# Attention and SwiGLU on one core: visits joined, products reordered, a third product in banks of its own

## The chip, the core and the metric

The kernel runs on one core of a Trainium2 chip. The core has a matrix engine (TensorE, PE in the profile), two engines for vectors (VectorE, DVE, and ScalarE, ACT), a general engine (GpSimd, POOL), and a queue engine that only sends DMAs here (SyncE, SP). Products land in PSUM, eight banks that PE writes and VectorE and ScalarE read; everything else is in SBUF. The metric is the time of one execution on the device in microseconds (us), median over several runs. All arithmetic is in float32.

## The reference

Attention without a softmax, then a feed-forward block:

```python
kv = np.einsum('bhsd,bhse->bhde', k, v)            # per batch and head, 64 x 64
out = np.einsum('bhsd,bhde->bhse', q, kv)
rms = np.sqrt(np.mean(out * out, axis=-1, keepdims=True) + 1e-06)
out = out / rms * g_norm
x = out.transpose(0, 2, 1, 3).reshape(B * S, H * D) # 4608 tokens x 512
g = x @ w_gate                                      # 512 x 1536
val = x @ w_val
return (g / (1 + np.exp(-g)) * val) @ w_out         # 1536 x 512
```

There are 8 batches, 8 heads, 576 positions and a head size of 64. q, k and v are float32; the three weights arrive as 64-bit numbers.

## The kernel before

**Blocks.** The 4608 tokens are nine blocks of 512. Block n lies across batches n-1 and n, so its attention needs the kv of both. Blocks 0, 1 and 2 are computed one at a time (`alone`), blocks 3 to 8 in pairs (`Pair`). Block 0 loads and converts the weights as it goes and multiplies plainly (`plain_up`). From block 1 on, each large product is split into 2 x 2 quarters and computed as seven products of quarter size with sums around them (a Strassen scheme in Winograd's form); the numbers 1 to 7 in the code name these products. In the pairs the seven are split once more (`Inner`).

**Up and Down.** `Ffn.up` (line 1094) makes the gate and value products for block 1 and block 2. It has six units, one for each pair of weight columns (`Up`, j = 0 to 5), and unit j's last two products, 3 and 4, are done within unit j+1; `sequence` (line 700) gives that order. The last unit has no successor: `end` (line 733) does its 3 and 4. `Ffn.down` (line 1118) then does the seven products with w_out, in the order of line 1122, and between them the attention of the next block (`steps`). For the last pair, blocks 7 and 8, there is no next block. In `Up` a product is 8 matmul instructions (a float32 matmul is two of them), in `Down` 24.

**Banks.** Products go to three PSUM pools. `CHAIN` (line 629) tells which: 1, 6, 7 and 4 add up in one bank of b, 5 and 3 in one bank of c, 2 has a bank of a. After each product a method copies or adds the running sum out (`after1`, `after6` and so on; ScalarE copies b, VectorE adds a and c), and the next product on the same bank waits until that is done. a has one bank, b three, c two. The remaining pool, m_psum, has two banks and serves attention. `Up.after7` (line 709) first copies b on ScalarE and then lets VectorE add c to the copy; the Silu of the other half stands behind that copy on ScalarE.

**Attention beside the products.** A visit is a stretch of 64 x 64 matmuls put between two products. `kv` (line 359) multiplies k by v for one or two groups of heads: 72 matmul instructions a group. `heads` (line 423) multiplies q by kv; `half(i)` in `ahead` (line 1269) does 64 of them. In block 1's Up, `third` and `two_thirds` visit block 2's two groups after products (1, 7) and (3, 7), where (j, p) is unit j and product p. In block 2's Up, `ahead` (line 1253) prepares blocks 3 and 4: both groups of block 3 after (0, 1), group 0 of block 4 after (1, 7), block 3's half 0 after (2, 1) and half 1 after (3, 1), and group 1 of block 4 after (3, 7).

**Loads.** k, v and q of the blocks ahead share four tiles (`ld_pool`), so a load waits until an earlier tile has been used. `load_kv(g)` is four DMAs of 288 KB on SyncE, `load_quarters` 16 small ones for half of q. `ffn.sends` is a list of which up to ten are sent after each product. `place_x` (line 515) writes the transposed x by 16 DMAs; for block 2 half of these are ScalarE's.

**Order.** A scheduler orders the instructions of each engine when the kernel is built, by the program's order and its own estimate of when each is ready; it may bring one forward. It also gives out the buffers. `in_order` fixes the program's order: for PE in the whole of block 2 and in the pairs' Down, and for VectorE and ScalarE in block 2's Up. PE in block 1 and in the pairs' Up is left to the scheduler. `tc.issue_after(x)` puts what is inside behind x on x's engine.

**Pairs.** `Inner` has four groups g of products for each j. A copy (line 825) or an add takes each product out. `made3` (line 845) ends a j: it multiplies the two halves of h, and applies a Silu to the second one (line 854) between; it runs inside the next j's first group. `Pair.second_sums` makes sums of h for the second block on GpSimd while the first block is in Down.

**The end.** In Down, product 3 comes last and adds onto 5 in bank c. For block 8 (`self.final`) its two halves have separate banks, the halves are stored one after the other, and product 4's result is stored before.

Of the kernel before, what the change touches and what calls it, by code (L numbers as in the profile page):

```python
# [14 lines left out]
P = 128  # L15
# [3 lines left out]
def kernel(  # L19
# [210 lines left out]
    class Att:  # L230
# [125 lines left out]
                    )  # L356
                self.q.append(tile_.rearrange("p (j u) d -> p j (u d)", u=2))

        def kv(self, g, apart=False):


            if self.n == B:
                return
            if g == 0 or apart:
                self.kv_ps = [m_psum.tile([P, 2, D], F32, name="m") for _ in range(2)]
            for c in range(KT):
                for r in range(2):
                    k, v = self.k[2 * g + r], self.v[2 * g + r]
                    for u in range(2):
                        self.positions = nc.tensor.matmul(  # L370
                            self.kv_ps[r][u * D : (u + 1) * D, g, :], lhsT=k[:, u, c, :], rhs=v[:, u, c, :],
                            start=(c == 0), stop=(c == KT - 1),
                        )
            if g == 1 or apart:
                dst = kvs[self.n % 3].rearrange("p (g r) d -> p r g d", r=2)
                of = slice(g, g + 1) if apart else slice(0, 2)
                for r in range(2):
                    nc.scalar.copy(out=dst[:, r, of], in_=self.kv_ps[r][:, of])
# [304 lines left out]
    class Up(Quad):  # L683
# [14 lines left out]
            self.w = {1: b11, 2: b21, 3: b22, 6: t2, 5: t[0], 7: t[1], 4: t[2]}  # L698

        def sequence(self, last):  # L700
            return [(self, 1), (self, 5), (last, 4), (last, 3), (self, 6), (self, 2), (self, 7)]

        def operands(self, p, e, i):
# [1 line left out]

        def after2(self):
            add(nc.vector, self.s, self.ps["a"], self.s)

        def after7(self):
            self.u3 = self.piece(2)  # L710
            copied = nc.scalar.copy(out=self.u3, in_=self.ps["b"])

            with tc.issue_after(copied.ins):
                nc.scalar.activation(out=self.s, in_=self.s, func=ACT.Silu)
            added = add(nc.vector, self.u3, self.ps["c"], self.u3)

            owed, self.ffn.owed = self.ffn.owed, None
            if owed:
                with tc.issue_after(added.ins):
                    owed()  # L720
# [11 lines left out]

        def end(self):

            for p in (3, 4):
                self.multiply(p)
            self.ffn.ended = self.ffn.h_sums(self.j, 1, nc.vector)

# [13 lines left out]
    class Inner:  # L752
# [50 lines left out]
        def multiply(self, p):  # L803
            if p == 1:
                self.begin()
            name, first = CHAIN[p]
            if first:
                self.ps[name] = PSUMS[name].tile([P, 2, 2, P], F32, name=name)
            ps = self.ps[name][:, 0 : len(self.outers)]
            for i, o in enumerate(self.outers):  # L810
                self.ffn.multiplied = nc.tensor.matmul(  # L811
                    ps[:, i], lhsT=stream.use(self.ffn.n, self.j, o, p), rhs=self.operand(o, p),
                    start=first and i == 0, stop=True, skip_group_check=True,
                )
            if p in self.ADDED:
                e, q = self.ADDED[p]
                dst = self.dst[:, :, :, e, q]
                add(nc.vector, dst, ps, dst)
            else:
                e, q = self.MADE[p]  # L820
                dst = self.dst[:, :, :, e, q]
                if self.onto:
                    add(nc.vector, dst, ps, self.onto(e, q))
                else:
                    nc.scalar.copy(out=dst, in_=ps)  # L825
            if p in (2, 7, 3, 4):
                getattr(self, f"made{self.g}", lambda *_: None)(p, e, q)
            stream.pump()
# [16 lines left out]
        def made3(self, p, e, q):  # L845
            if p != 4:
                return
            h = h_both[:, :, 2 * self.j : 2 * self.j + 2]
            halves = lambda t: t.rearrange("p (b e) t -> p b e t", b=2)
            c11, c12, c21, c22 = (self.whole(*i) for i in ((1, 1), (3, 1), (3, 0), (1, 0)))  # L850

            engine = nc.gpsimd if self.j + 1 < NP else nc.vector
            mul(engine, h[:, :, :, 0:HB], halves(c11), halves(c12))
            nc.scalar.activation(out=c21, in_=c21, func=ACT.Silu)
            mul(engine, h[:, :, :, HB:BLK], halves(c21), halves(c22))
            self.ffn.ended = self.ffn.a.h_sums(self.j, 1, engine)

# [119 lines left out]
    class Down(Quad):  # L977
        def __init__(self, ffn):
            super().__init__(NP)
            self.ffn = ffn  # L980
            self.t = {}
            self.final = ffn.n == NB - 1
            self.opens = None
            self.keeps = False
            if self.final:
                self.apart["c"] = None
# [13 lines left out]
                    )  # L1000
                self.t[p] += [t[:, 0], t[:, 1]]

        def multiply(self, p):
            super().multiply(p)
            if p in self.t and not self.keeps:
                stream.free(("T", p))
            if p == 7 and self.opens:
                stream.enable(self.opens)
            stream.pump()

        def order(self, p):
            order = [(e, i) for e in range(2) for i in range(self.steps)]
# [13 lines left out]
        def turn_s3(self):  # L1026

            pairs = self.ffn.h.rearrange("p (j e) t -> p e j t", e=2)
            sub(nc.vector, pairs[:, 0, :, 0:HB], pairs[:, 0, :, HB:BLK], pairs[:, 1, :, HB:BLK])

        def after2(self):
            add(nc.vector, self.o1[:, :, 0:HD], self.ps["a"], self.s)
            if self.final:
                self.ffn.store(self.o1[:, :, 0:HD], 0, slice(0, HD))

            pairs = self.ffn.h.rearrange("p (j e) t -> p e j t", e=2)
            self.s4 = sub(nc.vector, pairs[:, 1, :, 0:HB], pairs[:, 1, :, 0:HB], pairs[:, 0, :, HB:BLK])

        def after7(self):
            o = ring()  # L1040
            self.o1, self.o2 = o[:, 0:2], o[:, 2:4]
            u3 = self.piece(2)
            nc.scalar.copy(out=u3, in_=self.ps["b"])
            self.add_c(self.o2[:, :, HD:DM], u3)
# [21 lines left out]
    class Ffn:  # L1066
# [51 lines left out]
        def down(self, nxt, then={}):  # L1118

            down = self.down_  # L1120
            fill = nxt.steps() if nxt else {}
            for p in (1, 6, 5, 7, 2, 4, 3) if 5 in fill else (1, 5, 6, 7, 2, 4, 3):
                if p == 1 and 7 not in down.t:
                    down.turn_t(7, self.ended)
                if p == 6 and 4 not in down.t:
                    down.turn_t(4, nxt.halves[0] if nxt and nxt.n >= TURNED else None)

                with tc.issue_after(nxt.multiplied.ins) if self.n == 0 and p in (5, 6) else ExitStack():
                    down.multiply(p)
                self.make(12)  # L1130
                if p in fill:
                    fill[p]()
# [7 lines left out]
                if p == 1:  # L1140

                    with tc.issue_after(nxt.q_turned.ins) if self.n == 0 else ExitStack():
                        down.turn_s3()

        def plain_up(self, f, halves=(0, 1)):

# [95 lines left out]
    load_weights(4)  # L1242
    squared, scaled = blocks[0].first()

    def visit(ffn, att, gs, apart=False):

        with tc.issue_after(ffn.multiplied.ins):
            for g in gs:
                att.kv(g, apart)
        if att.n < B:  # L1250
            ffn.visited = att.positions

    def ahead(ffn, att, then):
# [8 lines left out]
        def turn(i):  # L1262
            ffn.chores.append(lambda: att.turn_q(i))

        def second():
            visit(ffn, then, (0,), True)
            ffn.sends.append(lambda: then.load_kv(1))

        def half(i):
            with tc.issue_after(ffn.multiplied.ins):  # L1270
                att.heads(i, range(NS), (m_psum, m_psum))
            ffn.visited = att.multiplied
            ffn.chores += att.chores(i)
            if i:
                ffn.chores += att.turn_steps()

        def rest():
            for i in range(2):
                load(then, i)()

        def raw():
            for j in range(2, NP):
                ffn.sends += raw_steps(j)

        def sums():
            ffn.chores.extend(att.sum_steps())

        for j in (NP - 2, NP - 1):
            ffn.making.extend(kept_steps(j, chunks(h_alone[:, NF - 4 :]) if j == NP - 1 else chunks(xi_alone)))

        return {
            (0, 1): first, (1, 6): lambda: turn(0), (1, 7): second, (2, 1): lambda: half(0), (2, 6): lambda: turn(1),
            (2, 7): rest, (3, 1): lambda: half(1), (3, 7): lambda: visit(ffn, then, (1,), True), (4, 1): att.place_x,
            (4, 2): raw, (5, 5): att.gain_x, (5, 6): sums,
        }

    def alone(n):
# [27 lines left out]
        elif n == 1:  # L1325

            def third():
                visit(ffn, nxt, (0,))
                nxt.load_kv(1)

            def two_thirds():
                visit(ffn, nxt, (1,))
                for i in range(2):
                    nxt.load_q(i)

            ffn.up({(1, 7): third, (3, 7): two_thirds})
            nxt.turn()
            for g in range(2):
                blocks[PAIRED].load_kv(g)
        else:  # L1340
            with in_order(nc.vector.engine, nc.scalar.engine):
                ffn.up(ahead(ffn, nxt, blocks[PAIRED + 1]))
# [8 lines left out]
            with tc.issue_after(nxt.scaled.ins):  # L1351
                blocks[PAIRED].inner_sums()

        ffn.down(nxt, {7: inner_sums} if n == 2 else {})
        if n == 0:
            blocks[2].load_kv(0)

            with tc.issue_after(nxt.halves[0].ins):
                for j in range(NP // 2):
# [69 lines left out]
```

## Time and profile before

| What | Value |
|---|---|
| Time, median of 3 runs | 1017.61 us (1016.21 to 1017.73) |
| Profiled execution, own time | 1018.16 us |
| its span, first to last instruction | 1016.4 us |
| PE: waits for another engine after 140 us, together | some 5 us |
| Block 1 Up and Down, about | 157 to 272 us |
| Block 2 Up and Down, about | 272 to 392 us |
| Pairs (3, 4), (5, 6), (7, 8) | 392 to 602, 602 to 810, 810 to 1016 us |
| SyncE: transfers on its queue | 138.20 MB, 50.3% of the 16 DMA engines |

The profile describes one execution. Its times are counted from the first instruction. A row of a timeline gives the start, the time until the last of the merged instructions ends, the engine, the line in the kernel, the operation, what it writes and reads, the shape and the count; a bracket says how long the engine stood idle before it and who released it. Many operations are recorded at the line of a small helper (lines 130 to 132 are add, sub and mul), so they are told apart by the tiles they touch. PE's busy time is modelled from a pipeline: two matmuls of one product start 0.216 us apart, though each row says 0.38.

### The profile page before, as it was taken

The page shows a single profiled execution, that of the slowest core. Times are in us where ns is not written, and L with a number is a line of the kernel's source. Part 1 is how long each engine was busy: PE and PEld are TensorE (multiplying, and loading weights), DVE is VectorE, ACT ScalarE, POOL GpSimd, SP SyncE. Part 2 cuts the span into 40 slices and gives each one's busy share as a digit, 9 for nine tenths or more (in the row PEclk, how much of TensorE's full clock was granted, in tenths as well). Part 3 has the DMA queues.
Part 4 walks back from the last instruction along what each step waited for, and adds up shares of the span by engine and source line. Part 5 has one row for each costly group of instructions (what it writes and reads, how often), then busy time and mean ns, then how long its engine had stood idle before and what let it go on. Part 6 is the DMA issues. An engine that isn't in the chain of part 4 may idle for free.

```text
span 1016.4 us, 17091 instructions
## 1 busy us (share of the span) xinstructions
PE 995.9 (98%) x6506; PEld 831.0 (82%) x6506; DVE 665.9 (66%) x1118; ACT 232.5 (23%) x367; POOL 368.3 (36%) x290
## 2 busy tenths in 40 slices
PE   5999999999999999999999999999999999999998
PEld 4544688888888888888888888888888888888887
DVE  2999797759767467656676746666668466666211
ACT  2666111221122211212212121121112121122000
POOL 0000273525444230445456004455660025546600
PEclk9999999999999999999999999999999999999999
DMA  8689643656665845766642364667221655452011
GB/s 220 198 263 270 125 79 132 219 166 145 170 144 109 224 94 157 190 175 176 165 139 43 109 165 133 183 164 191 75 43 42 147 164 154 142 156 84 1 42 42
DMA packets 254290, 143.23 MB, mean 141 GB/s; under 512 B 149504, under 2 KB 236544, under 8 KB 254208
## 3 DMA queue, kind: packets, MB, share of 16 engines
q1 hardware_dynamic: 223488, 138.20, 50.3%
q10 hardware_dynamic: 30656, 3.94, 2.4%
q8 instruction: 52, 0.85, 0.4%
q14 instruction: 30, 0.25, 0.1%
q0 software_dynamic: 64, 0.00, 0.0%
HBM read 104.99 MB, written 28.70 MB: 132 GB/s over the span
## 4 chain that ended last, share of the span: by engine, by line
PE 81%; DVE 8%; DMA 5%; ACT 1%; issue 1%; POOL 1%; SPq 1%; DVEq 0%; POOLq 0%; ACTq 0%
PE b L661 23%; PE b L811 21%; PE c L661 12%; PE c L811 10%; PE a L661 6%; PE a L811 5%; DMA ld<-in_moe_w_out_dram 2%; PE m L431 1%; PE m L370 1%; DVE r L190 1%; DVE arena L131 1%; DVE arena L199 1%; DMA arena<-in_v_dram 1%; SPq L333 1%; POOL t L131 1%
## 5 line engine op out<-in xcount | busy, mean ns | idle before, releaser
L811 PE MATMUL b<-arena,t 128*128 128x256 f32 x1008 | 244.5, 381 | 0.0
L811 PEld LDWEIGHTS b<-arena,t 128*128 128x128 f32 x1008 | 190.0, 190 | 29.6 <-DVE r L130 2.4
L130 POOL TENSOR_TENSOR r<-r 128x256 f32<-128x256 f32 (+1 forms) x90 | 94.8, 1054 | 246.4 <-DMA t<-w 149.4
L130 DVE TENSOR_TENSOR r<-b,r 128x512 f32<-128x512 f32 (+1 forms) x234 | 139.0, 607 | 60.3 <-PE b L811 55.4
L130 DVE TENSOR_TENSOR r<-c,r 128x512 f32<-128x512 f32 (+1 forms) x170 | 104.7, 624 | 108.0 <-PE c L811 41.3
L131 POOL TENSOR_TENSOR t<-wo 128x512 f32<-128x512 f32 x54 | 76.6, 1440 | 175.8 <-DVE wo L130 104.6
L132 POOL TENSOR_TENSOR arena<-r 128x1024 f32<-128x1024 f32 (+1 forms) x54 | 100.8, 1882 | 105.8 <-DVE r L130 81.4
L130 DVE TENSOR_TENSOR r<-a,r 128x512 f32<-128x512 f32 x93 | 59.2, 637 | 110.7 <-PE a L661 73.6
L811 PE MATMUL c<-arena,t 128*128 128x256 f32 x504 | 122.5, 379 | 1.0 <-ACT r L825 0.8
L131 DVE TENSOR_TENSOR arena<-arena 128x512 f32<-128x512 f32 (+3 forms) x96 | 103.2, 1090 | 18.1 <-PE b L661 14.0
L811 PEld LDWEIGHTS c<-arena,t 128*128 128x128 f32 x504 | 95.6, 190 | 14.7 <-ACT r L825 1.2
L661 PE MATMUL b<-wo,arena 128*128 128x256 f32 x432 | 98.3, 382 | 0.4 <-issue 0.3
L661 PE MATMUL b<-t,arena 128*128 128x256 f32 x432 | 96.4, 379 | 1.4 <-POOL s L130 0.7
L661 PEld LDWEIGHTS b<-t,arena 128*128 128x128 f32 x432 | 81.9, 190 | 13.2 <-POOL s L130 1.1
L661 PEld LDWEIGHTS b<-wo,arena 128*128 128x128 f32 x432 | 81.2, 190 | 12.7 <-DVE arena L132 0.9
L825 ACT COPY r<-b 128x512 f32<-128x512 f32 x54 | 31.6, 585 | 191.5 <-PE b L811 191.5
L131 POOL TENSOR_TENSOR t<-arena 128x512 f32<-128x512 f32 x36 | 51.4, 1438 | 59.4 <-DMA w<-t 23.3
L811 PE MATMUL a<-arena,t 128*128 128x256 f32 x252 | 66.1, 379 | 0.0
L811 PEld LDWEIGHTS a<-arena,t 128*128 128x128 f32 x252 | 47.9, 190 | 6.5
L661 PE MATMUL c<-wo,arena 128*128 128x256 f32 x216 | 48.2, 379 | 0.2 <-DVE r L130 0.2
L661 PE MATMUL c<-t,s 128*128 128x256 f32 x216 | 48.1, 379 | 0.0
L661 PE MATMUL a<-wo,arena 128*128 128x256 f32 x216 | 48.1, 379 | 0.0
(105 smaller groups left out, 1224.2 us busy)
## 6 DMA issues: line engine op xcount, KB each, us to landing
t<-w SPq DMA_DIRECT2D x180, 256.0 KB, 3.1
out_dram<-r SPq DMA_DIRECT2D x17, 512.0 KB, 2.9
ld<-in_k_dram SPq DMA_DIRECT2D x26, 288.0 KB, 5.4
ld<-in_v_dram SPq DMA_DIRECT2D x26, 288.0 KB, 5.9
t<-w SPq DMA_DIRECT2D x54, 128.0 KB, 2.2
ld<-in_moe_w_gate_dram SPq DMA_DIRECT2D x12, 512.0 KB, 4.8
ld<-in_moe_w_val_dram SPq DMA_DIRECT2D x12, 512.0 KB, 4.6
ld<-in_moe_w_out_dram SPq DMA_DIRECT2D x12, 512.0 KB, 5.0
```

The source lines that it names most:

```text
L130: add = lambda e, o, a, b: e.tensor_tensor(out=o, in0=a, in1=b, op=OP.add)
L131: sub = lambda e, o, a, b: e.tensor_tensor(out=o, in0=a, in1=b, op=OP.subtract)
L132: mul = lambda e, o, a, b: e.tensor_tensor(out=o, in0=a, in1=b, op=OP.mult)
L190: return nc.vector.scalar_tensor_tensor(out=mag, in0=mag, scalar=3, in1=sign, op0=OP.logical_shift_left, op1=OP.bitwise_xor)
L199: return nc.vector.tensor_tensor(out=dst.bitcast(U32), in0=self.mag.rearrange("p (a b) -> p a b", a=a, b=b), in1=unit.bitcast(U32).rearran ...
L333: queue.dma_start(out=to[32 * r : 32 * (r + 1), j, g0:g1], in_=q[b, 4 * i + 2 * j + h, s0 : s0 + 32 * (g1 - g0), 32 * d : 32 * (d + 1)].re ...
L370: self.positions = nc.tensor.matmul(self.kv_ps[r][u * D : (u + 1) * D, g, :], lhsT=k[:, u, c, :], rhs=v[:, u, c, :], start=(c == 0), stop= ...
L431: self.multiplied = nc.tensor.matmul(self.ps[i][u][p : p + D, t, j, :], lhsT=self.qt[rows, tile_t, head, p : p + D], rhs=kvs[b % 3][rows, ...
L661: self.ffn.multiplied = nc.tensor.matmul(banks[e][:, e], lhsT=lhsT, rhs=rhs, start=first and i == 0 and (e == 0 or banks[0] is not banks[1 ...
L811: self.ffn.multiplied = nc.tensor.matmul(ps[:, i], lhsT=stream.use(self.ffn.n, self.j, o, p), rhs=self.operand(o, p), start=first and i == ...
L825: nc.scalar.copy(out=dst, in_=ps)
```

## The change

1. **Visits joined.** In block 1 both groups of block 2's kv are done in one visit after (1, 7), both groups' k and v are sent for in block 0, and q after that one visit. In block 2, group i of block 4's kv is done directly behind half(i), after (2, 1) and (3, 1), in one bank of a and one of b; k and v of group 1 are sent for after (2, 1).
2. **k and v of block 3** are sent for in two steps: group 0 where both were, group 1 in block 1's Down after product 5, behind `place_x`.
3. **The last weight pair (j = 5)** of blocks 1 and 2: the sequence becomes 1, 5, (last 4), 6, (last 3), 7, 2, and `end` does 4 and then 3. The Silu moves from `after7` to `after2` for this unit.
4. **Blocks 7 and 8** (`lone`): Down's order becomes 1, 5, 6, 2, 7, 3, 4, with product 3 in banks of m_psum. VectorE adds product 5 to u2 after product 6. For block 8, product 3 is cut: its first half before 4, its second half behind it. The output tile is taken in `after2`.
5. **Pairs' Up:** the second Silu of `made3` is put behind the latest ScalarE copy of a product 5 (`fifth`).

```diff
-        def kv(self, g, apart=False):
+        def kv(self, g, apart=False, pools=None):
...
             if g == 0 or apart:
-                self.kv_ps = [m_psum.tile([P, 2, D], F32, name="m") for _ in range(2)]
+                self.kv_ps = [pool.tile([P, 2, D], F32, name=pool.name[0]) for pool in pools or (m_psum, m_psum)]
...
         def sequence(self, last):
+            if self.j == NP - 1:
+                return [(self, 1), (self, 5), (last, 4), (self, 6), (last, 3), (self, 7), (self, 2)]
             return [(self, 1), (self, 5), (last, 4), (last, 3), (self, 6), (self, 2), (self, 7)]
...
         def after2(self):
             add(nc.vector, self.s, self.ps["a"], self.s)
+            if self.j == NP - 1:
+                nc.scalar.activation(out=self.s, in_=self.s, func=ACT.Silu)
...
-            with tc.issue_after(copied.ins):
-                nc.scalar.activation(out=self.s, in_=self.s, func=ACT.Silu)
+            if self.j < NP - 1:
+                with tc.issue_after(copied.ins):
+                    nc.scalar.activation(out=self.s, in_=self.s, func=ACT.Silu)
...
-            for p in (3, 4):
+            for p in (4, 3):
                 self.multiply(p)
...
-                    nc.scalar.copy(out=dst, in_=ps)
+                    copied = nc.scalar.copy(out=dst, in_=ps)
+                    if p == 5:
+                        self.ffn.fifth = copied
...
-            nc.scalar.activation(out=c21, in_=c21, func=ACT.Silu)
+            with tc.issue_after(self.ffn.fifth.ins):
+                nc.scalar.activation(out=c21, in_=c21, func=ACT.Silu)
...
+        def third(self, es):
+
+
+            if es[0] == 0:
+                tiles = [m_psum.tile([P, 2, HB], F32, name="m") for _ in range(1 + self.final)]
+                self.thirds = tiles[0], tiles[-1]
+            for e in es:
+                for i in range(self.steps):
+                    lhsT, rhs = self.operands(3, e, i)
+                    self.ffn.multiplied = nc.tensor.matmul(
+                        self.thirds[e][:, e], lhsT=lhsT, rhs=rhs, start=i == 0 and (e == 0 or self.final),
+                        stop=i == self.steps - 1, skip_group_check=True,
+                    )
+            if not self.final:
+                add(nc.vector, self.o1[:, :, HD:DM], self.thirds[0], self.u2)
+                self.ffn.store(self.o1, 0)
+                return
+            for e in es:
+                add(nc.vector, self.o1[:, e, HD:DM], self.thirds[e][:, e], self.u2[:, e])
+                self.ffn.store(self.o1[:, e : e + 1, HD:DM], e, slice(HD, DM))
+
+        def after6(self):
+            super().after6()
+            if self.lone:
+                self.add_c(self.u2, self.u2)
...
-            for p in (1, 6, 5, 7, 2, 4, 3) if 5 in fill else (1, 5, 6, 7, 2, 4, 3):
+            down.lone = nxt is None
+            order = (1, 6, 5, 7, 2, 4, 3) if 5 in fill else (1, 5, 6, 7, 2, 4, 3)
+            if down.lone:
+                order = (1, 5, 6, 2, 7, 3, 4)
+            for p in order:
...
-                    down.multiply(p)
+                    down.multiply(p, *[(0,)] * (p == 3 and down.lone and down.final))
...
+            if down.lone and down.final:
+                down.multiply(3, (1,))
...
-        def second():
-            visit(ffn, then, (0,), True)
-            ffn.sends.append(lambda: then.load_kv(1))
-
         def half(i):
             with tc.issue_after(ffn.multiplied.ins):
                 att.heads(i, range(NS), (m_psum, m_psum))
-            ffn.visited = att.multiplied
+            visit(ffn, then, (i,), True, (a_psum, b_psum))
             ffn.chores += att.chores(i)
             if i:
                 ffn.chores += att.turn_steps()
+            else:
+                ffn.sends.append(lambda: then.load_kv(1))
...
             def third():
-                visit(ffn, nxt, (0,))
-                nxt.load_kv(1)
-
-            def two_thirds():
-                visit(ffn, nxt, (1,))
+                visit(ffn, nxt, (0, 1))
                 for i in range(2):
                     nxt.load_q(i)
 
-            ffn.up({(1, 7): third, (3, 7): two_thirds})
+            ffn.up({(1, 7): third})
             nxt.turn()
-            for g in range(2):
-                blocks[PAIRED].load_kv(g)
+            blocks[PAIRED].load_kv(0)
...
+        def second_kv():
+            with tc.issue_after(nxt.placed.ins):
+                blocks[PAIRED].load_kv(1)
+
-        ffn.down(nxt, {7: inner_sums} if n == 2 else {})
+        ffn.down(nxt, {1: {5: second_kv}, 2: {7: inner_sums}}.get(n, {}))
         if n == 0:
-            blocks[2].load_kv(0)
+            for g in range(2):
+                blocks[2].load_kv(g)
```

## What the change will do to the time

> **What bounds the kernel now.** I began with the page's first part.
>
> ```profile
> span 1016.4 us, 17091 instructions
> PE 995.9 (98%) x6506; PEld 831.0 (82%) x6506; DVE 665.9 (66%) x1118; ACT 232.5 (23%) x367; POOL 368.3 (36%) x290
> ```
>
> TensorE (PE) sets the time; the chain of waits agrees, 81% of it is PE, and the granted clock is 0.999. The change removes no product, so it can only win time in which PE stands or changes its way of working. The waits of PE after 140 us, i.e. behind the weight loading, are few:
>
> ```profile
> PE c L661 <- DVE r L130: 2.1, 3, 1.4
> PE c L811 <- ACT r L825: 0.8, 1, 0.8
> PE b L661 <- POOL s L130: 0.7, 1, 0.7
> PE b L661 <- ACT r L681: 0.7, 1, 0.7
> ```
>
> Each line: who waited for whom, total us, times, longest. These four are what the reordering aims at. What no view of waits counts is the slack around a visit (the small 64x64 matmuls of attention between products). For that I read the timeline of PE alone, where eight matmuls of one product start 1.73 us before the next product.
>
> ```profile
> 271.51 1.89 PE L661 MATMUL b<-arena 128*128 128x256 f32 x8
> 273.33 2.33 PE L370 MATMUL m<-ld 64*64 64x64 f32 x144
> 275.59 1.99 PE L661 MATMUL c<-arena,t 128*128 128x256 f32 x8
> 277.42 1.89 PE L661 MATMUL b<-arena 128*128 128x256 f32 x8
> ...
> 321.12 1.89 PE L661 MATMUL b<-arena,t 128*128 128x256 f32 x8
> 322.94 1.28 PE L370 MATMUL m<-ld 64*64 64x64 f32 x72
> 324.15 1.99 PE L661 MATMUL b<-arena 128*128 128x256 f32 x8
> 325.98 1.89 PE L661 MATMUL c<-arena,t 128*128 128x256 f32 x8
> ```
>
> From 271.51 to 277.42 are 5.91 us; two products take 3.45, so a visit of 144 costs 2.46. By the same sum the visit of 72 costs 4.86 - 3.45 = 1.41. The line through both: 14.6 ns a matmul and **0.36 us fixed for each visit**, whatever its length. The 64 matmuls of half() at 311.29 cost 1.29 by the same reading, where the line gives 1.29.
>
> **Visits joined.** Block 1: two visits of 72 (177.0 and 202.6) become one of 144: 2 x 1.41 - 2.46 = 0.36 saved. Block 2: kv visits of 72 at 294.8 and 322.9 join half()'s 64 at 297.9 and 311.3: 0.36 each, if passing from the 64 to the 72 is free. Both are 64x64 work, so at least the change of shape is not paid (the Trainium skill, "TensorEngine Tiling (Array Packing)", Key Properties, lets only a change of tiling mode drain the array; no row here has the two side by side); a wait for another bank there is not in this trace (nearest row: heads of two bank pairs in sequence at 122 us, where the next one waited 0.18 us on VectorE). Bounds of the three joins 0.5 to 1.1; I take **1.06**.
>
> What the joins need: in block 2 the kv results move from m_psum (held by half()) into one bank of a_psum and one of b_psum. Bank a was emptied by after2's add two products earlier (3.45 us; the add takes 0.69) and is wanted again at the next product 2, four products or 6.9 us later; the two ACT copies took 0.33. Of b's three banks units use two. So nothing there; without this cover the next product 2 would wait about 0.4. ACT takes these copies ahead of the squares, which start about 1.1 us later than now relative to half(). VectorE's chores follow them, and half(1) needs m_psum back only at the scale at 308.7, 2.6 us before it: enough.
>
> **The load that loses its lead.** kv(1) of block 4 was used at 322.94 and is now used right behind half(1). On the old clock half(1) starts at 311.29 - 1.41 (first visit gone) + 1.05 (72 x 14.6 ns joined before) = 310.93, and the 72 begin at 312.0. The load:
>
> ```profile
> 305.22 1.24 SPq L312 DMA_DIRECT2D ld<-in_v_dram  x2
> ...
> ld<-in_v_dram SPq DMA_DIRECT2D x2, 288.0 KB, 6.1
> ```
>
> The second v is issued at about 305.9 and lands 6.1 us later (DMA view of that stretch), at **312.0: no lead left**. SyncE's queue was full before it (32 q issues from 280.2 to 301.4, four w sends to 303.6), so its being sent one product later in the program should not move it: what it waits for now, the joined first visit, ends at 298.6. The Trainium skill ("DMA: Bandwidth & Descriptors", section "Anatomy of one DMA", fitted on POOL's path) prices a DMA at 2.0 us plus its bytes over 436 GB/s: as an estimate, four times 288 KB from 303.6 would be in at 308.3, 3.7 us early, and the edit free. This trace disagrees (6.1 us for one v; other transfers fill the engines at that time), and I take the row: 0.2 us of standing, bounds 0 and 3. SyncE then does 32 q issues in 20.0 us (306.5 to 326.5) and place_x. Relative to PE place_x comes at most 0.7 us later; gain_x began 0.8 us before product 5 ended at 339.8, and behind it ACT has 1.7 us until product 7 needs its copy. Covered.
>
> Loads of block 1: k and v of block 2, all eight DMAs, already went out at 119.5 to 124.7 and q from 180.3, ahead of their place in the program; these edits cost nothing. k and v (1) of block 3: four issues, 2.5 us of SyncE, move from 232.5 to behind place_x, which ends at 257.3. They delay the w sends at 257.3 by 2.6; SyncE idles from 261.4 to 266.9, so that ends there. Landing at about 266, use at 273.3: free.
>
> **Last weight pair.** Today the end is 7, 3, 4: product 3 adds into bank c, which VectorE may only read after ACT has copied product 7.
>
> ```profile
> 349.25 0.69 DVE L130 TENSOR_TENSOR r<-c,r 128x512 f32<-128x512 f32 x1 [0.38 <-ACT r L711]
> 349.99 1.99 PE L661 MATMUL c<-arena 128*128 128x256 f32 x8 [1.40 <-DVE r L130]
> ```
>
> Product 7 starts at 346.70 and Down's product 1 at 353.55: 6.85 for three products of 5.18, so 1.67 lost (idle plus a slow restart). In block 1 from 226.35 to 237.72 there are 48 matmuls of 215.8 ns, 10.36, and 0.09 of switching: 0.92 lost, since the scheduler had filled part with four matmuls of Down. With 7, 2, 4, 3 the copy (0.8 after product 7) lies beside product 2 (1.73), and VectorE's add (1.5) beside 2 and 4 (3.45). Late next is h: Down's product 1 needs the last h 4.3 us after product 3; add 0.7 and POOL's multiply 1.3, behind the one of product 4, come to about 3. The Silu moved into after2 runs on ACT within product 4. Gain **2.59**, bounds 1.5 and 2.6 (block 1's PE order is the scheduler's).
>
> **Blocks 7 and 8.** Products 6 and 7 share bank b, and 7 waits for the copy of 6:
>
> ```profile
> 991.40 0.58 ACT L681 COPY r<-b 128x512 f32<-128x512 f32 x1 [9.78 <-PE b L661]
> 992.03 5.45 PE L661 MATMUL b<-t,arena 128*128 128x256 f32 x24 [0.68 <-ACT r L681]
> ```
>
> From 986.02 to 997.32 two products take 11.30 in place of 10.36: 0.94. Block 7: 948.80 to 960.12, 11.32: 0.96 (the page names POOL, but ACT's copy at 954.18 is the last). In the order 1, 5, 6, 2, 7, 3, 4 every two products on b have another bank's product between (5.18 us, or half of product 3, 2.59). Added: one VectorE add behind product 6 (nearest row 0.69), beside product 2; product 3's h sum of 1.75 is beside product 7. The tail: the 512 KB store starts 1.8 us before the last matmul ends, lands in 2.8, so 1.0 after; the last add and 128 KB store start their packets later than that. The tail stays. Gain **1.90**, bounds 1.6 and 1.9.
>
> **Silu behind the copy.**
>
> ```profile
> 508.09 0.57 ACT L825 COPY r<-c 128x512 f32<-128x512 f32 x1
> 508.71 1.13 PE L811 MATMUL c<-arena,t 128*128 128x256 f32 x4 [0.75 <-ACT r L825]
> ```
>
> A Silu of 1.06 (507.13, L854) stood ahead of this copy. From 506.94 to 509.68 are eight matmuls, 1.73: 1.02 lost, at one place of 18. With the copy first, PE finds it done; the Silu ends at 508.8, before POOL is free for its second multiply. Gain **1.0**, bounds 0 and 1.0, as the scheduler may order this stage anew; its other gaps (0.76 near 432, 0.6 from 489 to 499) may come or go likewise.
>
> **The sum.** 1.06 + 2.59 + 1.90 + 1.0 - 0.2 = 6.35 us. Of the profiled execution's 1018.16 (span 1016.4 and 1.76 around it) that leaves 1011.8. That execution lies 0.55 over the median of 1017.61, so for the median I say **1011.3**.
>
> **Rivals.** (1) The load is late: a few of the 16 q issues of the next tile (0.63 each in the trace), already free to go, slip ahead of kv(1); five cost 3.1 us, and the time is 1014.2. For it: q of block 2 went out 22 us ahead of its program place. Against: kv(1) stands earlier in the program, and SyncE is backlogged. (2) The reordering does not take: the scheduler rearranges block 1 and the pair stage, and the one-place gains (0.92 and 1.0) are replaced by others: 1013.2. (3) The other side: all 32 q issues go ahead of kv(1). 20.0 us at SyncE, and PE, in program order here, stands as long: 1011.3 + 20 = 1031; it is slower from eleven issues on (11 x 0.63 = 6.9). Against: 16 of them need a tile that turn_q(1) frees only at 310.5.
>
> **How the numbers follow.** Forecast 0.62, rival (1) 0.17, rival (2) 0.13, rival (3) 0.04, anything else 0.04. The range takes 1010.0 (no late load, some of the pair's other gaps gone, 0.1% of scatter) to 1014.4, with rivals (1) and (2) in it. Faster by over 0.2% (about 2 us, what a measurement of this kernel can tell from none): 0.93, within 0.03, slower 0.04.
>
> **What would show it.** Right: no PE wait on DVE r L130 at the ends of blocks 1 and 2 and none on ACT r L681; one L370 group of 144 in block 1, and 72 straight behind 64 twice in block 2. Wrong: PE idle before L370 near 311 released by ld<-in_v_dram or in_k_dram, with q issues ahead of those loads at SyncE; or product 2 waiting for ACT L378.

## The result and the profile after

The changed kernel takes **1012.37 us** in the median of five runs (1011.12 to 1012.82), the kernel before beside it 1017.61 (1016.21 to 1018.82): a ratio of **0.9948, with a 95% interval of 0.9934 to 0.9963**, or 5.2 us. The profiled execution took 1012.7, its span 1010.9. The forecast was 1011.3, with a range of 1010.0 to 1014.4, in which the median lies.

The page of the changed kernel, its first part (busy time, share of the span, instructions):

```profile
span 1010.9 us, 17078 instructions
PE 993.7 (98%) x6506; PEld 831.6 (82%) x6506; DVE 673.7 (67%) x1121; ACT 232.2 (23%) x367; POOL 369.6 (37%) x290
```

PE's 6506 matmuls are all there still; only its standing and its changes of shape could shrink. The waits of PE behind the weight loading, by the same view as before (who waited for whom, total us, times, longest):

```profile
PE b L370 <- DMA ld<-in_v_dram: 0.6, 1, 0.6
PE m L431 <- DVE r L386: 0.6, 2, 0.3
PE c L661 <- DVE r L130: 0.2, 1, 0.2
```

The waits that the change aimed at are gone; of the group `c L661 <- DVE r L130`, 2.1 before, there is left one of 0.2 near 151 us, at the end of block 0, at which the change did not aim. Two waits are new: one for the load that had lost its lead, which the prediction priced at 0.2, and one for VectorE's transposes in block 0, which it did not have at all.

The timeline of PE in the changed kernel where block 2 begins and where half(0) and half(1) lie (start, duration, engine, line, operation, tiles, shape, count):

```profile
270.58 1.89 PE L661 MATMUL b<-arena 128*128 128x256 f32 x8
272.40 2.35 PE L370 MATMUL m<-ld 64*64 64x64 f32 x144
274.67 1.99 PE L661 MATMUL c<-arena,t 128*128 128x256 f32 x8
...
293.77 1.89 PE L661 MATMUL b<-arena 128*128 128x256 f32 x8
295.59 1.16 PE L431 MATMUL m<-kv,r 64*64 64x64 f32 x64
...
297.75 1.99 PE L661 MATMUL c<-arena,t 128*128 128x256 f32 x8
...
310.03 1.16 PE L431 MATMUL m<-kv,r 64*64 64x64 f32 x64
311.01 0.29 PE L370 MATMUL a<-ld 64*64 64x64 f32 x4
311.93 0.27 PE L370 MATMUL b<-ld 64*64 64x64 f32 x2 [0.62 <-DMA ld<-in_v_dram]
```

The first join is clean: from the product before it (293.77) to the second one behind it (299.58, not shown) are 5.81 us, so that its 136 matmuls cost 2.36 by the prediction's sum; its line gives 2.35 for one visit of that length. At the second one, four matmuls into bank a start and the first into bank b waits for v. What PE loses there is called the **stand** from here on: the longest gap between two starts of this visit, less the usual 0.01. It is 0.83 us here; the bracket shows 0.62, since it counts from the modelled end of the matmul before. From SyncE's timeline and the DMA view of 303 to 307 us, the load that it waits for (the DMA row's last column is the median time from issue to landing):

```profile
305.00 1.24 SPq L312 DMA_DIRECT2D ld<-in_v_dram  x2
```

```profile
ld<-in_v_dram SPq DMA_DIRECT2D x2, 288.0 KB, 5.8
```

The second v, issued at 305.64, took 6.2 and landed at 311.8.

The ends of the last weight pairs are as meant. Block 2's, and the last two products on bank b of blocks 7 and 8 with what lies between, in PE's timeline:

```profile
346.03 1.89 PE L661 MATMUL a<-arena 128*128 128x256 f32 x8
347.76 1.89 PE L661 MATMUL b<-arena,t 128*128 128x256 f32 x8
349.49 1.89 PE L661 MATMUL c<-arena 128*128 128x256 f32 x8
351.21 5.13 PE L661 MATMUL b<-wo,arena 128*128 128x256 f32 x23
```

```profile
950.39 5.34 PE L661 MATMUL a<-wo,arena 128*128 128x256 f32 x24
955.57 5.34 PE L661 MATMUL b<-t,arena 128*128 128x256 f32 x24
960.75 5.34 PE L1032 MATMUL m<-wo,arena 128*128 128x256 f32 x24
```

The starts lie 1.73 and 5.18 us apart, which is 8 and 24 times 0.216: PE passes from product to product without a gap.

Where the time came from is best seen in a **ledger**: for the n-th matmul of PE, its time since the first matmul, minus the same in the kernel before. Each stage's entry is the change of this difference across the stage. "Again" is the changed kernel profiled a second time (its row among the experiments). Negative is won.

| Stage | Forecast | After | Again |
|---|---|---|---|
| start, weights | 0 | -0.19 | -0.95 |
| block 0, heads wait for transposes | 0 | +0.63 | +0.58 |
| block 1, two visits to one | -0.36 | -0.35 | -0.36 |
| block 1, last pair to Down | -0.92 | -1.11 | -1.11 |
| block 2, first join | -0.35 | -0.34 | -0.32 |
| block 2, second join and the stand | -0.15 | **+0.59** | **+1.20** |
| block 2, last pair | -1.67 | -1.67 | -1.66 |
| pair (3, 4), a wait for w | 0 | -0.33 | +0.12 |
| pair (5, 6), Silu behind the copy | -1.0 | -0.93 | -0.94 |
| blocks 7 and 8 | -1.90 | -1.91 | -1.90 |
| to the last matmul | -6.35 | -5.57 | -5.32 |

(Stages of which nothing is said differ by 0.02 or less.) 0.78 of the forecast is missing in the first profile. The second join alone accounts for 0.74. That the two come so near is luck in part: block 0's loss of 0.63 is made up by the start, the wait in pair (3, 4) and 0.19 more at the end of block 1, together 0.71.

### The profile page after: what moved, and what is told of

Read it like the earlier page. It is cut to its first block, busy times and chain, and to the rows that moved or that the text cites. A ratio compares the mean times of both kernels' runs of the same rounds, so it can differ in the third digit from the quotient of the medians.

```text
span 1010.9 us, 17078 instructions
## 1 busy us (share of the span) xinstructions
PE 993.7 (98%) x6506; PEld 831.6 (82%) x6506; DVE 673.7 (67%) x1121; ACT 232.2 (23%) x367; POOL 369.6 (37%) x290
## 4 chain that ended last, share of the span: by engine, by line
PE 75%; DMA 1%; POOL 0%; SPq 0%; issue 0%; DVE 0%; POOLq 0%
PE b L816 22%; PE b L661 20%; PE c L816 11%; PE c L661 9%; PE a L816 5%; PE a L661 5%; PE m L431 1%; PE m L1032 1%; PE m L370 1%; DMA ld<-in_v_dram 1%; POOL t L131 0%; SPq L312 0%; PE b L370 0%; PE b L431 0%; PE a L431 0%
## 5 line engine op out<-in xcount | busy, mean ns | idle before, releaser
L816 PE MATMUL b<-arena,t 128*128 128x256 f32 x1008 | 244.5, 381 | 0.0
L816 PEld LDWEIGHTS b<-arena,t 128*128 128x128 f32 x1008 | 190.1, 190 | 29.6 <-DVE r L130 2.4
L130 POOL TENSOR_TENSOR r<-r 128x256 f32<-128x256 f32 (+1 forms) x90 | 94.7, 1054 | 246.1 <-DVE r L130 154.9
L130 DVE TENSOR_TENSOR r<-b,r 128x512 f32<-128x512 f32 (+1 forms) x234 | 138.9, 606 | 60.1 <-PE b L816 54.8
L130 DVE TENSOR_TENSOR r<-c,r 128x512 f32<-128x512 f32 (+1 forms) x170 | 104.5, 623 | 81.9 <-PE c L816 40.1
L130 DVE TENSOR_TENSOR r<-a,r 128x512 f32<-128x512 f32 x93 | 59.2, 636 | 108.3 <-PE a L661 70.7
L816 PE MATMUL c<-arena,t 128*128 128x256 f32 x504 | 122.5, 379 | 0.0
L816 PEld LDWEIGHTS c<-arena,t 128*128 128x128 f32 x504 | 95.6, 190 | 13.5 <-issue 0.3
L661 PE MATMUL b<-wo,arena 128*128 128x256 f32 x432 | 98.1, 382 | 0.2
L661 PE MATMUL b<-t,arena 128*128 128x256 f32 x432 | 96.2, 379 | 0.0
L661 PEld LDWEIGHTS b<-wo,arena 128*128 128x128 f32 x432 | 81.2, 190 | 12.5 <-DVE arena L132 0.9
L661 PEld LDWEIGHTS b<-t,arena 128*128 128x128 f32 x432 | 82.1, 190 | 11.2
L830 ACT COPY r<-b 128x512 f32<-128x512 f32 x54 | 31.7, 586 | 189.9 <-PE b L816 189.9
L816 PE MATMUL a<-arena,t 128*128 128x256 f32 x252 | 66.1, 379 | 0.0
L816 PEld LDWEIGHTS a<-arena,t 128*128 128x128 f32 x252 | 47.9, 190 | 6.5
L661 PE MATMUL c<-t,s 128*128 128x256 f32 x216 | 48.1, 379 | 0.0
L661 PE MATMUL a<-wo,arena 128*128 128x256 f32 x216 | 48.1, 379 | 0.0
L661 PEld LDWEIGHTS a<-wo,arena 128*128 128x128 f32 x216 | 41.0, 190 | 5.6
```

The costliest lines, as they stand in the source:

```text
L130: add = lambda e, o, a, b: e.tensor_tensor(out=o, in0=a, in1=b, op=OP.add)
L661: self.ffn.multiplied = nc.tensor.matmul(banks[e][:, e], lhsT=lhsT, rhs=rhs, start=first and i == 0 and (e == 0 or banks[0] is not banks[1 ...
L816: self.ffn.multiplied = nc.tensor.matmul(ps[:, i], lhsT=stream.use(self.ffn.n, self.j, o, p), rhs=self.operand(o, p), start=first and i == ...
L830: copied = nc.scalar.copy(out=dst, in_=ps)
```

## The experiments

The theory at this point (A): the second join works, and the stand comes from a lead that is too short. kv(1) of block 4 lands when SyncE's queue lets it, whatever PE does, and PE comes to it about 0.8 us too early. The rival (B): joining itself costs this (the banks a and b, ScalarE's copies, the passing from the 64 to the 72), or the stand is worth nothing, because a wait removed there comes back behind. Kernels with a single execution ("one time") are judged by the ledger of their traces, not by that time.

**A later place (x1_late).** half(1) and the joined visit move from behind product 1 of unit 3 to behind product 5, which is the next one; the load stays where it is.

```
-            (3, 1): lambda: half(1), (4, 1): att.place_x, (4, 2): raw, (5, 5): att.gain_x, (5, 6): sums,
+            (3, 5): lambda: half(1), (4, 1): att.place_x, (4, 2): raw, (5, 5): att.gain_x, (5, 6): sums,
```

> Edit: half(1) and the kv visit joined to it are done one product later, after (3, 5) in place of (3, 1). Theory A (the 0.83 us that PE stands before the second k.v stretch near 311.9 is the landing of k and v of group 1, whose time SyncE's queue sets, whatever PE does): PE comes 1.73 us later to it, finds the data there, and the stand is gone; from there on every product is 0.85 earlier than in the changed kernel, and place_x, which waits for SyncE's own queue until 326.6, does not move; span 1010.0, time about 0.85 below the changed kernel's. Rival B (the stand belongs to the join itself, e.g. to the change of banks between the two stretches): it stays at about 0.8 and the span is 1010.9.

The median was 1011.60 (1010.89 to 1012.71), with a ratio to before of 0.9938 (0.9922 to 0.9955). Its waits of PE, and the load in SyncE's timeline:

```profile
PE m L431 <- DVE r L386: 0.3, 1, 0.3
PE c L661 <- DVE r L130: 0.2, 1, 0.2
```

```profile
303.93 1.25 SPq L312 DMA_DIRECT2D ld<-in_v_dram  x2
```

The wait for the load is gone. PE reaches the joined visit at 311.86, 7.9 us after the v issues began. From block 2's start to its end the ledger moves by -2.19, after the change by -1.42: **0.77 better**. The second join now pays 0.34, of which 0.15 comes back in two gaps of 0.08 near 342 us.

**The join undone (x5_apart).** kv(1) goes back to its own visit after (3, 7); all else stays.

```
-            visit(ffn, then, (i,), True, (a_psum, b_psum))
+            if i:
+                ffn.visited = att.multiplied
+            else:
+                visit(ffn, then, (0,), True, (a_psum, b_psum))
...
-            (3, 1): lambda: half(1), (4, 1): att.place_x, (4, 2): raw, (5, 5): att.gain_x, (5, 6): sums,
+            (3, 1): lambda: half(1), (3, 7): lambda: visit(ffn, then, (1,), True, (a_psum, b_psum)), (4, 1): att.place_x, (4, 2): raw, (5, 5): att.gain_x, (5, 6): sums,
```

> Edit: in block 2 the second visit is taken apart again: half(1) alone after (3, 1), group 1 of block 4 after (3, 7). Theory A: one change of shape more, 0.36 us, and no stand: the products behind it are 0.83 - 0.36 = 0.5 us earlier than in the changed kernel. Rival B': joining is worth more than 0.83 and they come later.

One time of 1012.79. Block 2 moves by -2.00: 0.58 better than the changed kernel, with no stand. So this join, as placed, costs more than the visit that it saves. The whole was no faster in this one time; its profile lost 1.49 in block 0, of which more below.

**A shorter queue (x4_queues).** The place of the join stays; 8 of the 32 q issues ahead of the load go to ScalarE's queue.

```
-        def load(att, i):
-            return lambda: ffn.sends.extend(att.quarter_steps(i, (0, 1), (nc.sync,)))
+        def load(att, i, queues=(nc.sync,)):
+            return lambda: ffn.sends.extend(att.quarter_steps(i, (0, 1), queues))
...
-            ffn.sends += [load(att, 0), lambda: then.load_kv(0), load(att, 1)]
+            ffn.sends += [load(att, 0), lambda: then.load_kv(0), load(att, 1, (nc.sync, nc.scalar))]
```

> Edit: of the 32 q issues of block 3 in block 2's Up, eight go from SyncE to ScalarE's queue; nothing else. Theory A: SyncE comes 8 x 0.6 = 4.7 us earlier to k and v of group 1 (issue near 299 in place of 303.5), they land near 307, and PE's stand of 0.83 before the second k.v stretch is gone; ScalarE issues up to five in a row (0.45 each, 2.2 us) ahead of a copy that PE needs 3.45 us after, so PE does not wait there. Rival C (the landing is set by the DMA engines' load, not by the queue's order): issue early, landing still near 311 to 312, stand unchanged.

One time of 1011.70. SyncE's timeline:

```profile
299.24 2.04 SPq L312 DMA_DIRECT2D ld<-in_k_dram  x2
301.38 1.25 SPq L312 DMA_DIRECT2D ld<-in_v_dram  x2
```

The load is issued 3.6 us earlier, its second v lands at 308.2, and the stand is gone; block 2 moves by -2.17, 0.75 better. The same join in the same place and banks costs nothing once the load is early: **B's price of the joining itself falls**, and so does C, by which the landing would have stayed. One expectation failed: PE was not to wait for ScalarE. In ScalarE's timeline, five issues in a row took 3.95 us, where 2.2 had been thought:

```profile
283.69 3.95 ACTq L333 DMA_DIRECT2D ld<-in_q_dram  x5
287.68 0.58 ACT L677 COPY r<-b 128x512 f32<-128x512 f32 x1 [5.03 <-DMA ld<-in_q_dram]
```

In the changed kernel this copy of bank b starts at 283.61. The next product on b starts at 288.32, and the ledger loses 0.18 there.

**Block 1 in its old order (x2_block1).** If part of the stand is block 1's gain, block 1's loss should give it back.

```
-            if self.j == NP - 1:
+            if self.j == NP - 1 and self.ffn.n != 1:
...
-            for p in (4, 3):
+            for p in (3, 4) if self.ffn.n == 1 else (4, 3):
```

> Edit: the old order of the last weight pair (7, then 3, 4) for block 1 alone; block 2 keeps the new one. Theory A: about 0.9 to 1.1 us is lost again at the end of block 1, PE then comes that much later to the second k.v stretch of block 2, whose data land at an unmoved 311.9, and the stand of 0.83 there shrinks to 0 to 0.1; behind it the products are only 0.1 to 0.4 us later than in the changed kernel. Rival B (the stand is a fixed cost of the join): the 0.83 stays and everything behind is 0.9 to 1.1 later.

One time of 1012.92. Its waits of PE:

```profile
PE c L661 <- DVE r L130: 1.8, 2, 1.6
PE m L431 <- DVE r L386: 0.2, 1, 0.2
```

The expected sizes were missed. Block 1 lost 1.60 against the changed kernel, where about 1 had been thought: the wait at its end is 1.58 here and 0.51 in the kernel before, with the same four matmuls of Down ahead of it, because PE comes 0.6 earlier and VectorE's add of c 0.5 later (230.38 for 229.88). The stand shrank from 0.83 to 0.26, not to 0.1 or less, and behind block 2 there was 1.05 of the 1.60 left. That number alone would be B's; that the stand took up the rest is A's and not B's. **A gain upstream of a fixed landing is in part spent again as waiting at the landing.**

**Block 2's joins alone (y1_joins).** The kernel before, with the two joins and nothing else: block 1 keeps its old time, so PE comes to kv(1) late again.

```
-                self.kv_ps = [m_psum.tile([P, 2, D], F32, name="m") for _ in range(2)]
+                self.kv_ps = [pool.tile([P, 2, D], F32, name=pool.name[0]) for pool in pools or (m_psum, m_psum)]
...
-            ffn.visited = att.multiplied
+            visit(ffn, then, (i,), True, (a_psum, b_psum))
...
```

> The kernel before with block 2's two joins and nothing else: block 1 keeps its two visits of 72 and its late block end, so TensorE begins block 2 at about 273.3 on SyncE's clock instead of 272.4. k and v (1) of block 3 stay one load, as before. Theory A (the stand in the changed kernel is block 1's gain, which SyncE's queue does not follow): the second v lands where it did, TensorE comes 0.9 later than in the changed kernel, and the stand of 0.83 is gone or at most 0.2; from the start of block 2 to the last weight pair TensorE gains 0.5 to 0.7 on before. Theory B (the order of SyncE's instructions alone sets the stand): 0.8 of standing before the second k.v stretch all the same, and a net of -0.1 to 0.1 in block 2. One time for the whole: A 0.6 below before, B no change; one execution cannot tell these, the ledger of the trace can.

PE's and SyncE's timelines of this kernel:

```profile
313.57 0.29 PE L370 MATMUL a<-ld 64*64 64x64 f32 x4
313.77 0.27 PE L370 MATMUL b<-ld 64*64 64x64 f32 x2
```

```profile
306.84 1.25 SPq L312 DMA_DIRECT2D ld<-in_v_dram  x2
```

The stand is 0.11 in place of 0.83. B's stand of 0.8 does not come; A's does. Block 2's joins win 0.44 here, a little less than A's 0.5 to 0.7: 0.32 the first and 0.12 the second. The one time, 1018.8, is 1.8 above the kernel before beside it, so by itself it speaks for neither. The ledger, which stands against the first profile of before, has +1.01 by the heads of block 0 and +0.27 at the end of block 1, both ahead of the joins.

Put together, the profiles with the joined visit at (3, 1) and the 32 q issues on SyncE agree with A. The **lead** is the time from the start of the v issues to the first matmul of the joined visit:

| Kernel | v issued | PE there | lead | stand | sum |
|---|---|---|---|---|---|
| again | 304.80 | 310.70 | 5.90 | 1.18 | 7.08 |
| after | 305.00 | 311.01 | 6.01 | 0.83 | 6.84 |
| x3_fifth | 305.49 | 311.52 | 6.03 | 0.81 | 6.84 |
| x6_lone | 303.77 | 310.27 | 6.50 | 0.42 | 6.92 |
| x2_block1 | 305.27 | 311.88 | 6.61 | 0.26 | 6.87 |
| y1_joins | 306.84 | 313.57 | 6.73 | 0.11 | 6.84 |

The stand is 6.85 less the lead within 0.07, but for the first row. There the second v landed later, 7.07 after the v issues began, for 6.8 to 6.9 in the others: the time of the transfer scatters too. x1_late (lead 7.93), x1_again (7.22, with v issued at 305.08, as in the changed kernel) and x4_queues (9.47) have no stand. In x1_again that was close: the second v landed 7.20 after the v issues began, less than 0.1 us before PE came.

**The Silu's order undone (x3_fifth).**

```
-            with tc.issue_after(self.ffn.fifth.ins):
```

> Edit: the order behind the fifth product's copy is taken away; in the whole program one pair of ScalarE's instructions changes places by it, the Silu and the copy of bank c in the first pair's last weight pair. Theory: the products behind that place (near 496) come 0.9 us later, 0.75 of it as a wait of PE on ScalarE's copy, and nothing else changes. Rival: the wait was an accident of timing and does not come back: 0 to 0.2.

One time of 1013.91. Its wait of PE (L816 is the product that was L811, L830 the copy that was L825):

```profile
PE c L816 <- ACT r L830: 0.8, 1, 0.8
```

One pair of ScalarE's instructions changes places against the changed kernel, the other engines keep their order, and the stage's 0.93 is lost whole.

**Banks of blocks 7 and 8 undone (x6_lone).**

```
-            down.lone = nxt is None
+            down.lone = False
```

> Edit: blocks 7 and 8 go back to the old order of Down, with product 3 on bank c. Theory: product 7 waits for ScalarE's copy of product 6 again, once in each block: 0.95 each, 1.9 in all, and the tail behind the last product is as long as in the changed kernel to 0.1. Rival: the tail of the changed kernel is longer, because the 512 KB store goes out later, and part of the 1.9 is given back: 1.0 to 1.5.

One time of 1013.24. Its waits of PE behind block 6:

```profile
PE b L661 <- POOL s L130: 0.7, 1, 0.7
PE b L661 <- ACT r L681: 0.7, 1, 0.7
```

Both are back, and the ledger stays at -5.00 from there to the last matmul, where the changed kernel wins 1.91. The tail, by VectorE's last add, first in x6_lone, then in the changed kernel:

```profile
1008.15 0.42 DVE L130 TENSOR_TENSOR r<-c,r 128x256 f32<-128x256 f32 x1 [2.17 <-PE c L661]
```

```profile
1007.58 0.42 DVE L130 TENSOR_TENSOR r<-m,r 128x256 f32<-128x256 f32 x1 [7.35 <-PE m L1032]
```

To the ends of the spans, 1011.5 and 1010.9, both have 3.3 us: the other order of the last block adds nothing to the tail.

**The two versions side by side (again, x1_again).** The changed kernel and x1_late once more, beside each other.

> Edit: none, the changed kernel once more, beside the next one on the same chip. Near 0.9948 of the time of before; in its profile the stand before the second k.v stretch of block 2 is 0.6 to 1.0 again, and the wait of block 0's heads on VectorE (0.63 in the first profile) differs between profiles, since no instruction up to there has changed its place.

> Edit: that of x1_late, once more, to be compared with the changed kernel on the same chip. Theory A: 0.8 us below it, ratio to the time of before lower by 0.0008; a difference of this size can drown in the scatter of the timed runs, but the profile shows no stand.

| Kernel | Median (range) | Ratio to before, 95% |
|---|---|---|
| changed, again | 1013.21 (1011.02 to 1014.09) | 0.9951 (0.9939 to 0.9963) |
| x1_again | 1011.51 (1011.07 to 1013.13) | 0.9942 (0.9931 to 0.9954) |

The stand came again at 1.0 of idle time in the one and was absent in the other; block 2 moves by -0.78 and -2.04. By the traces, behind product 5 is the better place, with little to spare in x1_again; the timed intervals overlap, so that x1_late beats the changed kernel as a whole is likely and not shown.

**The kernel before, profiled again (before_again).**

> The kernel before, profiled a second time, for the 0.63 us that the changed kernel lost in block 0, where no instruction changed place. If that is scatter between executions (theory A), the same kernel shows other waits of the heads on VectorE's transposes than in its first profile, by 0.1 to 1.5 us. If it belongs to the change (theory B), block 0 repeats within 0.1 us. No other stage should differ by more than 0.3.

1017.42 in one time. Block 0 repeats to 0.00, so the expectation of A failed, and the wait in pair (3, 4) differs by -0.20 from the first profile, so that entry of the ledger is scatter. At the end of block 1 it stands 0.27 longer, as in y1_joins: a gap of PE in Down is 0.75 here and 0.48 in the first profile. Block 0's loss is another matter: both profiles of the kernel before show none, the ten of the other kernels 0.04 to 1.49. Yet y1_joins, whose instructions on all engines are those of the kernel before up to block 2, in order and waits, shows 0.71. So no instruction of the change makes it; why the kernel before had none twice stays open. What happens in it is seen in VectorE's and POOL's timelines, before and then after:

```profile
115.47 1.76 DVE L130 TENSOR_TENSOR s<-arena 128x1536 f32<-128x1536 f32 x1
```

```profile
107.43 7.38 POOL L131 TENSOR_TENSOR t<-wo 128x512 f32<-128x512 f32 x6 [104.58 <-DVE wo L130]
```

```profile
115.36 2.40 DVE L130 TENSOR_TENSOR s<-arena 128x1536 f32<-128x1536 f32 x1
```

```profile
108.74 7.40 POOL L131 TENSOR_TENSOR t<-wo 128x512 f32<-128x512 f32 x6 [105.89 <-DVE wo L130]
```

POOL's six products end at 114.81 before and at 116.14 after, 0.78 us into VectorE's sum; the sum takes 0.64 longer, and the transposes behind it, for which the heads wait, come 0.52 later. POOL waits for VectorE's last step on the weights, which ends 1.31 later, and the weights themselves are late: in SyncE's timeline three of their last issues took 6.28 us in place of 4.77.

## Why the prediction was right, and where its sum was off

- **Mechanisms.** All parts did what was said but for the second join of block 2, and the waits aimed at went. None of the rivals came. Of the first sign of being wrong one half came (PE idle before L370 near 311, released by v), but not the other, q issues of the next tile ahead of the load. Those 16 q issues stayed behind kv(1) in SyncE's timeline (rivals 1 and 3), and the scheduler gave the gains of block 1 and the pair stage (rival 2).
- **Terms that held.** Block 1's joined visit 0.35 for 0.36 (and nothing in y1_joins, which lacks it), the first join of block 2 0.34 for 0.35, block 2's last pair 1.67 for 1.67, blocks 7 and 8 1.91 for 1.90, the Silu 0.93 for 1.0. x3_fifth and x6_lone lose the last two again when undone. Block 1's last pair gave 1.11 for 0.92, as a gap of 0.48 that PE had in Down shrank to 0.29; against the second profile of the kernel before, where that gap is 0.75, it would be 1.38.
- **The mis-sized term** is "0.2 us of standing" before kv(1). It measured 0.83, and 1.18 in the second profile. The landing was right: 312.0 was forecast, and PE goes on at 311.93. PE's arrival was wrong: it was reckoned "on the old clock" from 311.29, with only block 2's own first join taken off, and so put at 312.0; PE was there at 311.01. The joined visit and the last pair of block 1, which the same text booked as gains of 0.36 and 0.92, bring block 2 forward (272.40 for 273.33, with block 0's loss against them), and were not carried into the lead. SyncE's queue did not come along: its v issues start at 305.00 for 305.22, with ten of the q issues taking 7.4 us in place of 6.4. With both gains taken off, the prediction's own sum puts PE at 310.7, as an estimate, and the stand near 1.3; PE came at 310.70 in the second profile, where the stand was 1.18. y1_joins, with block 1's old time, stands 0.11, as the prediction's sum would have it; x2_block1 stands 0.26. The bounds of 0 to 3 held it.
- **The rule weighed against the row.** The estimate by the Trainium skill's page "DMA: Bandwidth & Descriptors" (section "Anatomy of one DMA") would have had the edit free, even with PE 1.0 us earlier. The row's 6.1 us, 5.8 here, decided, and rightly.
- **The second join**, 0.35 by the forecast, is worth 0.12 (y1_joins) to 0.34 (x1_late, before its two small gaps). That passing from the 64 to the 72 is free holds at the first join; at the second, gaps of 0.04 between banks a and b remain.
- **The median.** The forecast left 6.3 us, the runs 5.2. Block 0's 0.63 is in the profile and not of the change, and medians of the changed kernel lie 0.8 apart between its two sets of runs, and the second profile of the kernel before is 0.81 shorter than its first; so how much of it is scatter can't be said. The stand, which both profiles show and three edits remove, is the cause that the runs do show: its stage falls short of the forecast by 0.74 in the first profile and by 1.35 in the second.

## What to carry to other kernels

A transfer's lead is the time from its issue to the arrival of the engine that uses it. It must not be shorter than the time from issue to landing, and the arrival must be reckoned with every gain that the same change books upstream; where the queue does not come forward with the engine, such a gain is spent waiting at the landing. A visit of small matmuls between large ones has a fixed price (here 0.36 us), so joining two saves that much, if the data of the later one is there at the earlier time; where it is not, a place one product (1.73 us) later won 0.77 here. Between two products on one bank, put a product on another one that is at least as long as the copy that takes the first one out.

## What was not expected of the hardware

VectorE's sum of two SBUF tiles does not share with POOL: the later of the two waits. In nine of the twelve profiles the sum started within the last product of POOL's run of multiplies. This product ended, for instance, 0.15, 0.47, 0.51, 0.74, 0.78 us after that start (x1_again, x1_late, again, y1_joins, after), and the sum, 1.76 in the kernel before, where POOL was done, took 1.77, 2.09, 2.13, 2.35, 2.40. What is added is the overlap less 0.14, within 0.01. x5_apart shows the lock from both sides. There the sum started 0.56 before the end of POOL's last product but one and took 2.18, 0.42 longer; POOL's last product met the running sum and took 2.78 in place of 1.26:

```profile
115.37 2.18 DVE L130 TENSOR_TENSOR s<-arena 128x1536 f32<-128x1536 f32 x1
```

```profile
109.77 8.91 POOL L131 TENSOR_TENSOR t<-wo 128x512 f32<-128x512 f32 x6 [106.92 <-DVE wo L130]
```

The Trainium skill's page "SBUF — State Buffer" (section "SBUF: two separate sides") says of such a pair of instructions that the ports are an exclusive lock and the later one "fully blocks"; these rows agree, to the 0.14.

The same issue on the same queue has no fixed time: the ten q issues ahead of the load took 5.57 us in x6_lone, 6.37 before, 7.41 after and 7.49 in x1_again. A lead of 6.85 us that hangs behind 32 of these is not one to plan to the tenth.
